# One decode layer: the end of the program moves from SyncE to TensorE

## The chip, the core and the metric

The kernel runs on one core of a Trainium2 chip. The core has five instruction streams: TensorE (PE for its matmuls, PEld for its weight loads), VectorE (DVE), ScalarE (ACT), GpSimd (POOL) and SyncE (SP). A letter q behind a name, as in SPq, means the engine's sequencer: DMA issues, waits and semaphore instructions, which are not counted as busy time. The metric is the device time of one execution in microseconds (us).

## What is computed

The reference adds three things: the input row x, a windowed attention over cached keys and values, and a gated feed-forward layer. Both of the latter read the same normalized row.

```
xn = _layernorm(x)                                  # x: 1 x 1 x 1024
return x + _A_ref(xn, k_cache, v_cache, wq, wo)     # 32 heads of 128, 4 key/value heads
         + _B_ref(xn, w_gate, w_up, w_down)         # 1024 -> 3584 -> 1024, gelu(g) * u

# _A_ref: q = x @ wq; the last 4096 rows of the caches; softmax(q k^T / sqrt(128)) v; then @ wo
# _B_ref: h = gelu(x @ w_gate) * (x @ w_up); then h @ w_down
```

There is one token, so nearly all of the work is to read the weights and the cache window, 94 MB in 32-bit floats, and to multiply each of them once.

## The kernel before

SP reads the weights and caches into one ring of 32768 columns in SBUF, in the order wq, keys, values, w_gate, w_up, wo, w_down (the table `PLAN`, which also says whose place in the ring each transfer takes). TensorE and VectorE share the multiplication: some rows of each weight go through matmuls, the others through a multiply and add on VectorE (`add_scaled`). The last weight, w_down, comes in ever smaller pieces, and `downs` finishes the output from them. It adds the last matmuls to the sum in two halves, tiles `y` and `y_last`, and each half is written by two DMAs of 2 x 128 elements, four stores in all. Two of the stores are issued by SP and two by ACT. The last one of all, of the lower part of `y_last`, is issued by SP.

No scheduler stands between the code and the program. `Flow` records every operation with the tiles that it reads and writes, works out which semaphores each must wait for, and issues the operations in the order in which the code calls them (line 97 is an added wait, line 237 is the operation itself: every operation of the program stands at these two lines, so the profile is read by tile names). The semaphores of DMAs are named flow_d_ and the operation's number, those of engines flow_e_ and the engine. In the built program the four stores have the semaphores flow_d_861 (number 138, SP), flow_d_862 (139, ACT), flow_d_866 (140, ACT) and flow_d_870 (145, SP, the last).

Behind the last store, `finish` leaves all semaphores at zero for the next execution. It does so in five steps on one engine, SP. It waits until `mark`, the first addition into `y`, is done (by then nobody waits for the loads' semaphores any more), and clears the first 36 semaphores with one range clear (line 210). It waits for the three earlier stores (line 212), and clears the next ten with a second range clear (line 213). Then it waits for the last store and takes that store's 16 back (line 214). The order in the numbers comes from the constructor: loads that nobody needs any longer stand first, the last store's semaphore stands last.

Behind `finish` the program ends on each engine. What the runtime then does is not among the program's instructions.

Of the kernel before, what the change touches and what calls it, by code (L numbers as in the profile page):

```python
# [36 lines left out]
SIZES = {"tp": NB, "acc": 2 * NB, "part": 8 * NB, "rows": 2 * NB}  # L37


def bits(dims):  # L40
    total = 1
    for step, count in dims:
        if step:
            grown = 0
            for i in range(count):
                grown |= total << (step * i)
            total = grown
    return total


class Flow:
# [4 lines left out]
    def __init__(self, nc, plan=None):  # L56
        self.nc = nc
        self.plan, self.idle = plan or (None, [])
        self.ops = []
        self.touched = {}  # L60
        self.sems = {}
        if self.plan:
            inc = self.plan[-1][1]
            self.last = inc
            used = {key for waits, _ in self.plan for key, _ in waits}
            used.update(inc for _, inc in self.plan if inc is not None)
            rest = sorted(used - {*self.idle, inc})
            for key in [*self.idle, *rest, inc]:
                self.sem(key)
        self.first = None  # L70
        for name in ("tensor", "vector", "scalar", "gpsimd", "sync"):
            setattr(self, name, Queue(self, getattr(nc, name)))
# [6 lines left out]
    @staticmethod  # L79
    def place(access):  # L80
        tensor = access.bass_ap.tensor
        if tensor.space == bass.MemoryType.DRAM:
            return None
        row = math.prod(list(tensor.shape)[1:])
        dims = [tuple(x) for x in access.ap]
        first, col = divmod(access.offset, row)
        parts = bits([(step // row, count) for step, count in dims if step >= row]) << first
        rest = [(step, count) for step, count in dims if step < row]
        if tensor.space == bass.MemoryType.PSUM:
            return tensor.name, (1 << 128) - 1, bits_of_banks(bits(rest) << col)  # L90
        return tensor.name, parts, bits(rest) << col
# [106 lines left out]
    def finish(self, mark, stores):  # L198

        end = self.nc.sync
        if not self.plan:
            return
        numbers = [s.num for s in self.sems.values()]
        first, cut, last = min(numbers), min(numbers) + len(self.idle), max(numbers)
        assert numbers == list(range(first, last + 1))
        assert stores[-1] == len(self.plan) - 1
        end.wait_ge(self.sem(self.plan[mark][1]), self.ticks(mark))
        end.sem_clear(range(first, cut))  # L210
        for k in stores[:-1]:
            end.wait_ge(self.sem(("d", k)), 16)
        end.sem_clear(range(cut, last))
        end.wait_ge(self.sem(self.last), 16).then_inc(self.sem(self.last), -16)

# [649 lines left out]
```

## Time and profile before

| what | value |
|---|---|
| time, median of 3 runs | 226.24 us (226.08 to 226.28) |
| time of the profiled execution | 226.24 us |
| its span, from the first to the last instruction of the program | 224.9 us |
| around the span (the difference) | 1.3 us |
| PE, PEld, DVE, ACT, POOL busy | 124.4, 65.4, 112.2, 28.0, 2.8 us |
| read from HBM | 94.38 MB, 420 GB/s over the span |

The span begins with the first and ends with the last instruction of the program on any engine; the 1.3 us are what the time of the execution has beyond it. Idle time stands in brackets behind a row, with the work that ended it. Times within the span are in us from its start.

### The profile page before, as it was taken

Reading aid. Unit: us, or ns where it says so; the run is one execution under the profiler, and the core shown is the slowest. Engines: PE = TensorE matmul, PEld = TensorE weight load, DVE = VectorE, ACT = ScalarE, POOL = GpSimd, SP = SyncE. Lnnn points to the kernel's source line nnn. Section 1 sums busy time; section 2 is a strip of 40 time slices with the busy share of each in tenths; the row PEclk is TensorE's granted clock in tenths of the full one; section 3 lists DMA queues with packets and bytes.
Section 4 is the critical chain, followed back from the end, with each engine's and each line's share of the span. In section 5 each row is a group of like instructions: output and inputs, shape, how many; then the busy total and the mean of one; then the engine's idle time right before and its main releaser. Section 6 shows DMA issues by size and latency. Waiting matters only on the chain.

```text
span 224.9 us, 2512 instructions
## 1 busy us (share of the span) xinstructions
PE 124.4 (55%) x1107; PEld 65.4 (29%) x1107; DVE 112.2 (50%) x142; ACT 28.0 (12%) x54; POOL 2.8 (1%) x9
## 2 busy tenths in 40 slices
PE   0120900557799860989848562235308988700986
PEld 0010200102654710754711110001004986300442
DVE  7030920592235082245049589239708933990942
ACT  2030000002435500445500310000000000000000
POOL 3000000000000000000000000000000000010000
PEclk9999995587999998599976958559955755755599
DMA  9889889799997999999989999989989989999994
GB/s 373 374 373 560 373 373 560 321 426 463 439 490 338 417 455 446 396 468 428 472 350 454 423 459 439 479 388 420 481 385 443 478 385 461 434 396 396 426 403 172
DMA packets 3193, 94.53 MB, mean 420 GB/s; under 512 B 446, under 2 KB 718, under 8 KB 1040
## 3 DMA queue, kind: packets, MB, share of 16 engines
q1 hardware_dynamic: 3160, 94.38, 97.8%
q8 instruction: 8, 0.13, 0.2%
q10 hardware_dynamic: 24, 0.01, 0.0%
q14 instruction: 1, 0.01, 0.0%
HBM read 94.38 MB, written 0.00 MB: 420 GB/s over the span
## 4 chain that ended last, share of the span: by engine, by line
DMA 67%; DVE 20%; PE 9%; SPq 1%; ACT 1%; issue 1%; POOL 0%; DVEq 0%
DMA ring<-in_B_w_gate 26%; DMA ring<-in_A_wq 18%; DMA ring<-in_A_wo 13%; DVE part L237 13%; DMA ring<-in_B_w_down 10%; PE tp L237 6%; DVE out_part L237 3%; PE out L237 3%; DVE rows L237 2%; SPq L237 1%; DVE g_sb L237 1%; ACT kT L237 1%; DVE hz L237 1%; PE acc L237 0%; DVE kT L237 0%
## 5 line engine op out<-in xcount | busy, mean ns | idle before, releaser
L237 PE MATMUL acc<-ring,xz 128*32 128x512 f32 x176 | 33.1, 850 | 39.3 <-DMA ring<-in_A_wq 23.0
L237 DVE SCALAR_TENSOR_TENSOR part<-ring,xz,part 128x3584 f32<-128x3584 f32 (+1 forms) x9 | 37.2, 4130 | 22.0 <-DMA ring<-in_A_wq 12.5
L237 PE MATMUL tp<-ident,ring 128*128 128x128 f32 x128 | 20.5, 310 | 8.9 <-DMA ring<-in_A_k_cache 6.1
L237 PEld LDWEIGHTS acc<-ring,xz 128*32 128x32 f32 x176 | 7.2, 145 | 60.3 <-issue 26.3
L237 DVE SCALAR_TENSOR_TENSOR out_part<-ring,oz,out_part 128x1024 f32<-128x1024 f32 x16 | 20.6, 1285 | 0.6
L237 PE MATMUL out<-ring,hz 128*32 128x256 f32 x168 | 12.8, 466 | 13.9 <-DMA ring<-in_B_w_down 13.9
L237 PEld LDWEIGHTS tp<-ident,ring 128*128 128x128 f32 x128 | 15.4, 155 | 16.9 <-DMA ring<-in_A_k_cache 7.0
L237 DVE COPY kT<-tp 128x512 f32<-128x512 f32 x12 | 8.1, 690 | 19.9 <-PE tp L237 19.9
L237 PE MATMUL out<-ring,oz 128*32 128x256 f32 x120 | 10.9, 541 | 9.6 <-DMA ring<-in_A_wo 9.6
L237 ACT ACTIVATE kT<-tp 128x512 f32<-128x512 f32 x20 | 11.4, 595 | 26.9 <-PE tp L237 26.9
L237 PE MATMUL tp<-ident,kT 128*128 128x4 f32 (+4 forms) x64 | 13.4, 343 | 1.6 <-DVE hz L237 1.6
L237 PEld LDWEIGHTS tp<-ident,kT 128*128 128x128 f32 (+2 forms) x64 | 13.1, 294 | 2.2 <-DVE hz L237 1.8
L237 DVE TENSOR_SCALAR part<-ring,xz 128x3584 f32<-128x3584 f32 (+1 forms) x3 | 6.5, 2172 | 13.7 <-DMA ring<-in_A_wq 7.6
L237 PEld LDWEIGHTS out<-ring,hz 128*32 128x32 f32 x168 | 5.8, 131 | 20.8 <-DMA ring<-in_B_w_down 16.1
L237 PE MATMUL acc<-part,units 128*32 128x512 f32 x44 | 7.1, 731 | 7.2 <-DVE part L237 7.2
L237 DVE SCALAR_TENSOR_TENSOR out_part<-ring,hz,out_part 128x1024 f32<-128x1024 f32 x6 | 7.7, 1284 | 5.6 <-DMA ring<-in_B_w_down 5.5
L237 PEld LDWEIGHTS out<-ring,oz 128*32 128x32 f32 x120 | 5.2, 154 | 15.3 <-DMA ring<-in_A_wo 10.5
L237 PE MATMUL o<-ring,pT 128*32 128x128 f32 x256 | 8.0, 274 | 1.1 <-ACT pT L237 1.0
L237 DVE TENSOR_REDUCE m<-s 128x2 f32<-128x1024 f32 x4 | 4.9, 1224 | 6.1 <-PE s L237 6.1
L237 PE MATMUL s<-kT,qz 128*32 128x512 f32 x64 | 7.7, 598 | 0.0
L237 PEld LDWEIGHTS o<-ring,pT 128*32 128x32 f32 x256 | 6.8, 110 | 2.2 <-ACT pT L237 1.9
L237 PE MATMUL tp<-ident,x_rows 2*128 2x2 f32 x4 | 0.6, 252 | 10.3 <-DMA x_rows<-in_A_x 10.3
(96 smaller groups left out, 73.5 us busy)
## 6 DMA issues: line engine op xcount, KB each, us to landing
ring<-in_B_w_gate SPq DMA_DIRECT2D x2, 7168.0 KB, 29.4
ring<-in_A_k_cache SPq DMA_DIRECT2D x4, 2048.0 KB, 19.7
ring<-in_A_v_cache SPq DMA_DIRECT2D x2, 4096.0 KB, 26.8
ring<-in_B_w_up SPq DMA_DIRECT2D x2, 3584.0 KB, 21.6
ring<-in_B_w_up SPq DMA_DIRECT2D x1, 7168.0 KB, 26.0
ring<-in_B_w_down SPq DMA_DIRECT2D x2, 2048.0 KB, 21.4
ring<-in_B_w_down SPq DMA_DIRECT2D x2, 512.0 KB, 21.9
ring<-in_B_w_down SPq DMA_DIRECT2D x2, 256.0 KB, 21.9
```

The lines of the kernel that those rows point to most:

```text
L237: return lambda *a, **k: self.flow.issue(self.engine, lambda: call(*a, **k))
```

## The change

One engine's stream gets the end of another's. The five steps of `finish` are issued on TensorE in place of SP. Since SP issues the last store and the second range clear must not come ahead of that, there is a new semaphore, `ISSUED` (flow_s_0, number 145 in the changed program, and the last store's becomes 146). SP adds one to it behind its last store, and TensorE waits for it ahead of its second range clear, which now covers 11 semaphores, 135 to 145, in place of 10.

```
+ISSUED = ("s", 0)
...
-            for key in [*self.idle, *rest, inc]:
+            for key in [*self.idle, *rest, ISSUED, inc]:
                 self.sem(key)
...
-        end = self.nc.sync
+        end = self.nc.tensor
...
+        self.nc.sync.sem_inc(self.sem(ISSUED), 1)
         end.wait_ge(self.sem(self.plan[mark][1]), self.ticks(mark))
         end.sem_clear(range(first, cut))
         for k in stores[:-1]:
             end.wait_ge(self.sem(("d", k)), 16)
+        end.wait_ge(self.sem(ISSUED), 1)
         end.sem_clear(range(cut, last))
         end.wait_ge(self.sem(self.last), 16).then_inc(self.sem(self.last), -16)
```

These are SP's last instructions before the change: the last pieces of w_down, SP's two stores, and the two range clears (ISA) with what they and the waits ahead of them wait for. Instructions that only wait or only count are not rows of this listing, so the last wait of line 214 is not seen.

```order
L237 DMA ring<-in_B_w_down 128x1024 [waits flow_e_PE]
L237 DMA ring<-in_B_w_down 128x512 [waits flow_e_DVE]
L237 DMA ring<-in_B_w_down 128x256 x2
L237 DMA out_y<-y 2x128 [waits flow_e_DVE]
L237 DMA out_y<-y_last 2x128 [waits flow_e_DVE]
L210 ISA [waits flow_e_DVE]
L213 ISA [waits flow_d_866,flow_d_862,flow_d_861]
```

The same place on SP after the change (all line numbers are five higher):

```order
L242 DMA ring<-in_B_w_down 128x1024 [waits flow_e_PE]
L242 DMA ring<-in_B_w_down 128x512 [waits flow_e_DVE]
L242 DMA ring<-in_B_w_down 128x256 x2
L242 DMA out_y<-y 2x128 [waits flow_e_DVE]
L242 DMA out_y<-y_last 2x128 [waits flow_e_DVE]
```

SP's stream ends with its store and the count on `ISSUED` behind it. On TensorE, the program ended with the last matmuls of w_down:

```order
L237 MATMUL tp<-ring,hz 32x128 [waits flow_d_756]
L237 MATMUL tp<-ring,hz 32x128 x3
L237 MATMUL acc<-ring,hz 32x128 [waits flow_d_757]
L237 MATMUL acc<-ring,hz 32x128
L237 MATMUL acc<-ring,hz 32x128 [waits flow_d_758]
L237 MATMUL acc<-ring,hz 32x128
```

After the change the two range clears stand behind them, and the second one has four waits in place of three:

```order
L242 MATMUL acc<-ring,hz 32x128 [waits flow_d_757]
L242 MATMUL acc<-ring,hz 32x128
L242 MATMUL acc<-ring,hz 32x128 [waits flow_d_758]
L242 MATMUL acc<-ring,hz 32x128
L214 ISA [waits flow_e_DVE]
L218 ISA [waits flow_d_866,flow_s_0,flow_d_862,flow_d_861]
```

The four waits are spread over three instructions: one that waits for flow_d_866 alone, one for flow_s_0 and flow_d_862, and the range clear itself, which waits for flow_d_861. Nothing else in the order of any engine differs.

More of the change, by code (lines that the diff above doesn't have):

```diff
@@ L37 @@
 SIZES = {"tp": NB, "acc": 2 * NB, "part": 8 * NB, "rows": 2 * NB}
+ISSUED = ("s", 0)
 def bits(dims):
@@ L67, in __init__ @@
             rest = sorted(used - {*self.idle, inc})
-            for key in [*self.idle, *rest, inc]:
+            for key in [*self.idle, *rest, ISSUED, inc]:
                 self.sem(key)
@@ L198, in finish @@
     def finish(self, mark, stores):
-        end = self.nc.sync
+        end = self.nc.tensor
         if not self.plan:
@@ L208, in finish @@
         assert stores[-1] == len(self.plan) - 1
+        self.nc.sync.sem_inc(self.sem(ISSUED), 1)
         end.wait_ge(self.sem(self.plan[mark][1]), self.ticks(mark))
@@ L212, in finish @@
             end.wait_ge(self.sem(("d", k)), 16)
+        end.wait_ge(self.sem(ISSUED), 1)
         end.sem_clear(range(cut, last))
```

## The prediction

> **What bounds the kernel now.** I read the page's chain first, then the stretches, then the last three microseconds instruction by instruction. The chain, by engine and by line, and the busiest DMA queue say what the time goes to:
>
> ```profile
> DMA 67%; DVE 20%; PE 9%; SPq 1%; ACT 1%; issue 1%; POOL 0%; DVEq 0%
> q1 hardware_dynamic: 3160, 94.38, 97.8%
> ```
>
> The 16 DMA engines are busy for 97.8% of the span with SP's loads. The change touches none of these; it works behind the last store. So the second view is a table of three stretches (PE, PEld, DVE, ACT and POOL busy time with instruction counts, granted clock, DMA share, GB/s):
>
> ```profile
> 0.00:221.60 221.60, 122.67 (x1083) 64.84 (x1084) 110.91 (x138) 27.98 (x54) 2.79 (x9) 0.78 0.99 426
> 221.60:224.00 2.40, 1.70 (x24) 0.60 (x24) 1.24 (x4) 0.00 (x0) 0.00 (x0) 1.00 0.16 55
> 224.00:224.90 0.90, 0.00 (x0) 0.00 (x0) 0.00 (x0) 0.00 (x0) 0.00 (x0) 1.00 0.01 2
> ```
>
> Until 221.60 the kernel is bound by DMA (share 0.99). From 224.00 no engine computes and hardly a byte moves: 0.90 us of pure latency. There the change is at work, and in the 226.24 - 224.9 = 1.3 us that the time has beyond the span. The timeline shows what comes just before:
>
> ```profile
> 222.62 0.68 PE L237 MATMUL acc<-ring,hz 128*32 128x128 f32 x8
> ...
> 223.08 0.60 DVE L237 TENSOR_TENSOR y_last<-y,acc 64x128 f32<-64x128 f32 x2
> ...
> 223.46 0.28 ACTq L237 DMA_DIRECT2D out_y<-y_last  x1
> 223.71 0.26 SPq L237 DMA_DIRECT2D out_y<-y_last  x1
> ```
>
> TensorE is done at 222.62 + 0.68 = 223.30, VectorE at 223.68; SP has issued the last store at 223.97. What SP does then stands in its lines one by one (duration in ns, then the start in us), and the third row is its only wait there:
>
> ```profile
> L210 SPq EVENT_SEMAPHORE_RANGE_CLEAR  x1: 92/92/92, 224.0 to 224.0; - x1
> L212 SPq EVENT_SEMAPHORE  x1: 28/28/28, 224.7 to 224.7; - x1
> SPq L212 <- DMA out_y<-y_last: 0.5, 1, 0.5
> L213 SPq EVENT_SEMAPHORE_RANGE_CLEAR  x1: 42/42/42, 224.7 to 224.7; - x1
> L214 SPq EVENT_SEMAPHORE  x1: 17/17/17, 224.8 to 224.8; - x1
> ```
>
> So the first clear lies under the flight of the stores. SP waits 0.5 us for ACT's second store, clears ten semaphores, and the last store's landing ends the program. These rows are rounded to 0.1 us. The trace also keeps when each semaphore was written; its records, in ns from the start of the span, are these (2 is a semaphore that the program does not use, 3 to 53, 54 to 104, 105 to 155, 156 to 206 and 207 to 255 are zeroed in five blocks behind the program's end):
>
> ```
> 140 (ACT's second store, landed)      224636
> 145 (the last store, landed)          224821     taken back by SP  224855
> 135 to 144 (SP's second clear)        224732 ... 224746
> 2   before the first instruction      -371 -337 -299 -255 -231 -119 -80 -46 0
> 2   at the end                        223490 224403 224441 224485 225004 | 225048 225087 225121 225168
> 207 to 255 zeroed                     225127 ... 225214
> 7 to 53 zeroed                        225419 ... 225764
> 2   once more                         225988 226023 226061 226104 226128 | 226227 226265 226299 226346
> ```
>
> Semaphore 2 counts a meeting of the five engines, up and back down: nine updates each time. Who stands where is read from the program's first instructions, which follow the first meeting:
>
> ```profile
> L853 SPq DRAIN  x1: 7/7/7, 0.0 to 0.0; - x1
> L853 DVEq DRAIN  x1: 10/10/10, 0.1 to 0.1; - x1
> L853 POOLq INC_SWDGE_SEM  x1: 27/27/27, 0.1 to 0.1; - x1
> L853 ACTq DRAIN  x1: 8/8/8, 0.1 to 0.1; - x1
> L853 PEldq DRAIN  x1: 8/8/8, 0.3 to 0.3; - x1
> ```
>
> SP starts first and PE last. So I read the order as PE, ACT, POOL, DVE, SP going up, and DVE, POOL, ACT, PE coming back. At the end PE came to it at 223490, 0.19 us behind its last matmul; ACT, POOL and DVE follow at 224403 to 224485; SP, at the turn, comes at 225004, 0.15 us behind its last instruction. Only the way back, 164 ns to PE at 225168, is left then.
>
> **The change, step by step.** The sum is made against the profiled execution, 226.24 us, which is also the median shown.
>
> First clear, 36 semaphores. It leaves SP (92 ns) and goes to PE, which has been idle since 223.30. Its wait, for the first addition into `y`, was met at 222.74. Even at the slowest pace that the records show, (225764 - 225419) / 46 = 7.5 ns a semaphore, it takes 0.3 us and ends by 223.7, under the wait for ACT's store to 224.64. Cost: nothing; the cover is the 0.9 us of flight.
>
> `ISSUED`. SP adds one behind its store at 223.97: one instruction of 17 ns, seen by about 224.07. If SP had to wait for its store as ACT does on its way to the meeting (0.66 us from 223.74 to 224403), it would come at 224.63, still no later than ACT's landing. Cost: nothing, but the cover is then used up.
>
> PE's waits. How PE executes a wait is shown by the added waits in the program:
>
> ```profile
> L97 SPq EVENT_SEMAPHORE  x11: 17/17/17, 26.4 to 195.9; - x11
> L97 PEldq EVENT_SEMAPHORE  x8: 51/51/51, 10.2 to 219.9; - x8
> L853 SPq EVENT_SEMAPHORE  x1: 17/17/17, 0.7 to 0.7; - x1
> L853 PEldq EVENT_SEMAPHORE  x1: 51/51/51, 0.7 to 0.7; - x1
> ```
>
> 51 ns on PE against 17 on SP. The records give 29 ns from the write of a semaphore to PE's start (SP 17), and 76 ns from one wait's start to that of the next instruction. ACT's store lands at 224.636, so PE's first wait starts at 224.665, the second at 224.741, the clear at 224.817. On SP the clear started at 224.72, with one wait less ahead of it.
>
> The second clear. No row shows a range clear on PE. By SP's row it is 42 ns and costs nothing more; by the pace of 7.5 ns for 11 semaphores, plus SP's fixed 28 ns (42 less the 14 in which its ten are written) taken up to three times, 110 to 165 ns. I take 130, since 3 to 53 are the block that PE, the last one released, would zero. The last wait then starts at 224.98 with a short step between, and ends at 225.03. The last store has landed at 224.82, so it is no longer the last thing waited for. The span becomes 225.03 in place of 224.86: +0.17 (bounds +0.08 with SP's clear, +0.21 with the slow one).
>
> The meeting. PE now comes last, and it stands at the start of the way up. Its step from its last instruction to its arrival I take as 0.16 us, like SP's 0.15 and PE's own 0.19 behind its last matmul (bounds 0.15 and 0.22; the latter is 225764 to 225988). Then follows the whole way up and back: 0 - (-371) = 371 ns in the first meeting, 226346 - 225988 = 358 in the last; before, it was 164 of it. That is +0.19 to +0.21 us more. I take +0.20.
>
> Sum: 0.17 + 0.01 + 0.20 = +0.38 us, 226.24 + 0.38 = 226.62. The bounds add up to 0.08 + 0.00 + 0.19 = 0.27 and 0.21 + 0.07 + 0.21 = 0.49, thus 226.51 to 226.73. All of it is late next at PE's release, which already zeroed its block last, from 225419 to 225764.
>
> [...]
>
> **The rivals.** 0.2% of 226.24 us is 0.45 us, about what a measurement of this kernel can tell from no change; the forecast lies just under that.
>
> The end of the time does not hang on PE's release. If the time ends with something that only needs the last engine's arrival, the +0.20 is not paid, and the store's landing may even cover the clear: 226.24 + 0.08 to 0.17, about 226.3 to 226.4. Against it: the time ends 1.3 us behind the span, at a point past the zeroing that waits for the release.
>
> PE's end is dearer than SP's by more than the rows show: each of the five instructions at a price between its measured 51 ns and a slow clear, a longer step to the meeting, and the first steps of PE behind its release (251 ns from 225168 to 225419, SP's 123) paid again. One more such step of 0.1 to 0.25 us gives 226.7 to 226.9, over the bound. For it: PE has the slowest of every step in the records. It decides from 0.07 us beyond the forecast.
>
> The other side: SP is set free early. A fetch of instructions starts as SP comes to the meeting; the row has the queue's packets, MB and share, and the record of this one is a start at 225034 and a duration of 493 ns:
>
> ```profile
> q14 instruction: 1, 0.01, 0.0%
> ```
>
> If the fetch, done at 225.53, is what holds the last meeting, then SP, arriving at about 224.64, has it done 0.37 us earlier, and the time falls to 226.24 - 0.37 + 0.08 = 225.95. It decides only if something waits for the fetch beyond 225.53. Against it: PE's zeroing lasts until 225.76, after the fetch, and would be later.
>
> **How the numbers follow.** The forecast, up to the bound of 226.69: 0.48. The end that does not hang on the release, 226.25 to 226.45: 0.12. PE dearer, above 226.69: 0.34, a third of it beyond 226.9, since one unshown instruction form on the path may cost what no row bounds. SP set free: 0.06. The predicted time is the forecast's, 226.62. The range goes from 226.25 to 226.95; it leaves out the 0.06 below and about 0.10 above. Faster by over 0.2% is 0.06; within 0.2% is 0.48 + 0.12 = 0.60; slower is 0.34.
>
> **What would show it.** In the changed profile the second clear stands on PE at about 224.8, 0.1 us later than on SP, and takes over 100 ns. The last wait starts later than the last store's landing, and the span is about 225.0. PE's first clear ends before 224. SP's last row is its count at about 224.0. Semaphore 2 has no early update any more: PE writes the first of the nine, behind the end of the span, and 0.36 us pass from it to the last. The zeroing of 7 to 53 starts about 0.4 us later. The prediction is wrong if the clear on PE is as quick as on SP and the way up costs nothing (226.3), if PE takes much longer than 0.16 us to the meeting, or if anything ahead of 221.6 differs, since the change issues nothing there.

## The result, and the profile after

The change made the kernel slightly slower: 226.74 us at the median against 226.24 us before, a ratio of 1.0022 (95% interval 1.0014 to 1.0030). One execution of twelve took 348 us and is left out of the ratio; without it the median is 226.72. The profiled execution took 226.70 us, with a span of 225.1 us.

The table of stretches, now to 225.10 (columns as before), shows where the time did not come from. The 221.60 us under the loads are as they were, with a DMA share of 0.99. The stretch in which nothing computes grew from 0.90 to 1.10 us:

```profile
0.00:221.60 221.60, 121.75 (x1087) 64.22 (x1091) 110.91 (x138) 27.97 (x54) 2.80 (x9) 0.79 0.99 426
221.60:224.00 2.40, 1.62 (x24) 0.54 (x24) 1.22 (x4) 0.00 (x0) 0.00 (x0) 1.00 0.14 48
224.00:225.10 1.10, 0.00 (x0) 0.00 (x0) 0.00 (x0) 0.00 (x0) 0.00 (x0) 1.00 0.03 9
```

The timeline shows the same matmuls and stores, 0.06 to 0.08 us earlier in this execution:

```profile
222.54 0.68 PE L242 MATMUL acc<-ring,hz 128*32 128x128 f32 x8
...
223.40 0.28 ACTq L242 DMA_DIRECT2D out_y<-y_last  x1
223.63 0.26 SPq L242 DMA_DIRECT2D out_y<-y_last  x1
```

Line by line, the end of the program now stands on PE (duration in ns, then the start in us). SP's only instruction behind its store is the first row:

```profile
L212 SPq EVENT_SEMAPHORE  x1: 17/17/17, 223.9 to 223.9; - x1
L214 PEldq EVENT_SEMAPHORE_RANGE_CLEAR  x1: 305/305/305, 222.8 to 222.8; - x1
L216 PEldq EVENT_SEMAPHORE  x1: 51/51/51, 224.6 to 224.6; - x1
L217 PEldq EVENT_SEMAPHORE  x1: 51/51/51, 224.7 to 224.7; - x1
L218 PEldq EVENT_SEMAPHORE_RANGE_CLEAR  x1: 121/121/121, 224.8 to 224.8; - x1
L219 PEldq EVENT_SEMAPHORE  x1: 51/51/51, 225.0 to 225.0; - x1
```

The second range clear takes 121 ns on PE for 11 semaphores, where SP took 42 for ten, and the last wait starts at 225.0. The trace's records of semaphore writes and instruction starts give this to the nanosecond:

```
140 (ACT's second store, landed)    224582
PE: first wait, second wait, clear  224610, 224716, 224822 (ends 224943)
146 (the last store, landed)        224760
PE: last wait                       225034 (ends 225085)
2   at the end                      225314 225349 225387 225430 225454 | 225551 225589 225625 225672
7 to 53 zeroed                      225886 ... 226234
2   once more                       226458 226492 226530 226574 226598 | 226696 226734 226769 226815
```

The last store had landed 274 ns before PE turned to it. From there on all is late: PE comes to the meeting first of nine updates, and all of the way up and back follows.

Counted from the last store's landing, so that an earlier or later landing drops out, the time divides into five stages (ns). "End" is the end of the program's last instruction; "step" is from there to that engine's update of semaphore 2; "way" is from there to the last of the nine updates; "zeroing" is from there to the first of PE's zeroed semaphores; "rest" runs to the last of all updates. Which engine an update or a zeroed block belongs to is inferred. Five of the nine updates lie behind the program's last instruction where that is SP's, all nine where it is PE's. The block 7 to 53 (3 to 6 have no record) is taken as PE's: it starts last, and its 7.5 ns a semaphore are near the pace at which PE's own first range clear wrote its 36, (223090 - 222846) / 35 = 7.0, where SP's took (224098 - 224040) / 35 = 1.7.

| kernel | end | step | way | zeroing | rest | sum |
|---|---|---|---|---|---|---|
| before | 34 | 149 | 164 | 251 | 927 | 1525 |
| after | 325 | 229 | 358 | 214 | 929 | 2055 |

The difference is 530 ns, and the profiled landing was 61 ns earlier than before, which leaves 469. The times of these two executions differ by 0.46 us. In every profiled execution of this study the time is the last update of semaphore 2 less 0.10 to 0.12 us (before 226.24 against 226.346, after 226.70 against 226.815). So the time ends with the last meeting, and these stages account for what the change did between these two executions.

### The profile page after: what moved, and what is told of

Its sections match the earlier page's. It is cut to its first block, busy times and chain, and to the rows that moved or that the text cites. A ratio compares the mean times of both kernels' runs of the same rounds, so it can differ in the third digit from the quotient of the medians.

```text
span 225.1 us, 2514 instructions
## 1 busy us (share of the span) xinstructions
PE 123.4 (55%) x1107; PEld 64.8 (29%) x1107; DVE 112.1 (50%) x142; ACT 28.0 (12%) x54; POOL 2.8 (1%) x9
## 4 chain that ended last, share of the span: by engine, by line
DMA 67%; DVE 20%; PE 9%; SPq 1%; ACT 1%; issue 1%; POOL 0%; DVEq 0%
DMA ring<-in_B_w_gate 26%; DMA ring<-in_A_wq 18%; DMA ring<-in_A_wo 13%; DVE part L242 13%; DMA ring<-in_B_w_down 10%; PE tp L242 6%; DVE out_part L242 3%; PE out L242 2%; DVE rows L242 2%; SPq L242 1%; DVE g_sb L242 1%; ACT kT L242 1%; DVE hz L242 1%; PE acc L242 0%; DVE kT L242 0%
## 5 line engine op out<-in xcount | busy, mean ns | idle before, releaser
L242 PE MATMUL acc<-ring,xz 128*32 128x512 f32 x176 | 34.7, 883 | 42.7 <-DMA ring<-in_A_wq 23.6
L242 PE MATMUL acc<-part,units 128*32 128x512 f32 x44 | 5.8, 599 | 6.4 <-DVE part L242 6.4
```

Source lines behind the costliest of these rows:

```text
L242: return lambda *a, **k: self.flow.issue(self.engine, lambda: call(*a, **k))
```

## The experiments

Two theories were set against each other. By the first, the place of the last engine in the meeting costs, beside the speed of its instructions. By the second, PE's slow instructions are all. The table of stages for all kernels stands at the end of this section. The stages are read from one profiled execution of each kernel; the times are medians of all, each beside the kernel before on the same chip.

### Only the last wait on TensorE

SP keeps its waits and both range clears:

```
-        end.wait_ge(self.sem(self.last), 16).then_inc(self.sem(self.last), -16)
+        self.nc.tensor.wait_ge(self.sem(self.last), 16).then_inc(self.sem(self.last), -16)
```

> SP keeps both range clears and the three earlier waits; TensorE only waits for the last store and takes its 16 back. Theory 1 (the place in the meeting costs, whatever PE does before): the end of the span is 0.05 us later against the last store's landing than before (29 + 51 ns on PE in place of 17 + 17 on SP), PE's step to the meeting is 229 ns in place of 149, the way up and back 358 in place of 164, PE's release to its zeroing 214 in place of 251: +0.05 + 0.08 + 0.19 - 0.04 = +0.28 us, 226.52. Theory 2 (PE's slow waits and clears behind ACT's store are all of it): only the 0.05 remains, 226.3.

Measured: 226.52 against 226.24 us, ratio 1.0013 (1.0004 to 1.0022). PE has one instruction behind its matmuls:

```profile
L213 SPq EVENT_SEMAPHORE_RANGE_CLEAR  x1: 42/42/42, 224.6 to 224.6; - x1
L214 PEldq EVENT_SEMAPHORE  x1: 51/51/51, 224.7 to 224.7; - x1
```

The stages sum to 1811 ns, 286 more than before, where 0.28 us was expected. The span ends only 45 ns later against the landing. What is paid lies outside the span, where the page shows nothing: 86 ns in the step and 192 in the way. The theory that PE's slow chain is all of it falls.

### The late store waited for last

In the changed kernel the waits were put in another order. The wait that the code names first ends up in the range clear itself (flow_d_861 in the changed kernel), and the others in two instructions ahead of it. So ACT's second store, which lands last of the three, is now named first, and the two instructions ahead no longer wait for it:

```
-        for k in stores[:-1]:
-            end.wait_ge(self.sem(("d", k)), 16)
+        end.wait_ge(self.sem(("d", stores[2])), 16)
         end.wait_ge(self.sem(ISSUED), 1)
+        for k in stores[:2]:
+            end.wait_ge(self.sem(("d", k)), 16)
```

> The changed kernel with its waits in another order: the store that lands last of the three (ACT's second) is waited for by the range clear itself, the two others and ISSUED by the two waits ahead. Theory 1: the clear starts 29 ns behind that landing in place of 240, so that the chain is 0.21 us shorter and still just longer than the last store's flight: 226.74 - 0.21 = 226.53. If only the place in the meeting counts, and the chain does not: 226.74, no change to the changed kernel.

Measured: 226.52 against 226.24 us, ratio 1.0016 (1.0007 to 1.0025). The two waits start at 224.4 and 224.5, the clear at 224.6:

```profile
L218 PEldq EVENT_SEMAPHORE  x2: 51/51/51, 224.4 to 224.5; - x2
L219 PEldq EVENT_SEMAPHORE_RANGE_CLEAR  x1: 121/121/121, 224.6 to 224.6; - x1
L220 PEldq EVENT_SEMAPHORE  x1: 51/51/51, 224.8 to 224.8; - x1
```

The clear starts at 224.644, 59 ns behind the landing of ACT's second store in place of 240; 29 were expected, but the second wait starts at 224.538 and the clear follows it by 106. The program ends 115 ns behind the landing of the last store in place of 325. These 210 ns come from the order of the waits alone, and they come back in the time (226.74 to 226.52). Both shares of the loss are real: the chain of waits and the place in the meeting.

### The clears on TensorE, the last wait on SP

```
-        end.wait_ge(self.sem(self.last), 16).then_inc(self.sem(self.last), -16)
+        self.nc.sync.wait_ge(self.sem(self.last), 16).then_inc(self.sem(self.last), -16)
```

> TensorE has both range clears and the waits ahead of them, SP waits for its own last store and takes the 16 back. Theory 1: SP comes to the meeting as before, but PE, first on the way up, comes behind its clear: clear's end 183 ns behind the last store's landing, a step of 229, and 358 for the whole way, against 183 and 164 before: +0.42 - 0.04 = +0.38 us, 226.62. A theory by which the last wait on PE is what costs says no change, 226.24; one by which the end of the span decides says +0.15, 226.4.

Measured: 226.57 against 226.24 us, ratio 1.0016 (1.0007 to 1.0025). SP is done with the last store as early as before (end 34 ns behind the landing), yet the time is 0.33 us longer, because PE, at the foot of the way up, is still clearing:

```profile
L218 PEldq EVENT_SEMAPHORE_RANGE_CLEAR  x1: 121/121/121, 224.9 to 224.9; - x1
L219 SPq EVENT_SEMAPHORE  x1: 17/17/17, 224.8 to 224.8; - x1
```

The stages sum to 346 ns more than before, against 380 expected; PE's step behind a range clear was 193 ns, not 229. So the loss does not need the last wait on PE: it is enough that PE comes late to the meeting.

### The end on the three other engines

The changed kernel with `end` on ScalarE, GpSimd or VectorE:

```
-        end = self.nc.tensor
+        end = self.nc.scalar    # or gpsimd, or vector
```

> The changed kernel with ScalarE in place of TensorE. Theory 1 (place): ACT is second on the way up, 323 ns from the end of the meeting in place of SP's 164, thus +0.16 us, and its waits take 17 ns as SP's do, so that its chain ends with the last store's landing or up to 0.1 behind it: 226.40 to 226.50. Theory 2 (PE is slow, the place is free): 226.24 to 226.34.

> The changed kernel with GpSimd in place of TensorE. By the place in the meeting (third on the way up, 285 ns from there to the end in place of 164): +0.12 us and whatever its chain of waits ends behind the last store's landing, 0.0 to 0.15: 226.36 to 226.51. If only PE's slowness counts: 226.24 to 226.39.

> The changed kernel with VectorE in place of TensorE. By the place in the meeting (fourth on the way up, 241 ns from there to the end in place of 164): +0.08 us; its waits for two semaphores take 50 ns at a distance of 98, so its chain ends 0.1 to 0.25 us behind the last store's landing: 226.40 to 226.57. If the place is free: 226.34 to 226.49. The profile decides: the second half of the nine updates of semaphore 2, counted from VectorE's arrival, takes 241 ns or 164.

Measured: ScalarE 226.34 against 226.24 (ratio 1.0009, 1.0000 to 1.0018), GpSimd 226.81 against 226.17 (1.0026, 1.0015 to 1.0038), VectorE 226.48 against 226.17 (1.0013, 1.0004 to 1.0022).

The way from the last engine's arrival to the end of the meeting was 323 ns from ACT, 282 from POOL, 242 from DVE, 358 from PE and 164 from SP. It falls with the place on the way up, as the order PE, ACT, POOL, DVE, SP demands, and this order had been read from the program's start alone. The expected values were 323, 285 and 241. By the stages ACT costs 225 ns and DVE 235, within what was expected. By its median ACT was a miss: 226.34 lies below the expected 226.40 to 226.50, at the upper end of what the second theory gave (226.24 to 226.34), and only the interval (0 to 0.41 us) allows the 225 ns. What speaks for the place is the way of 323 ns, and the time beyond the span, 1.52 us on average against 1.36 (last column of the table). POOL was a miss: 652 ns in place of 120 to 270. Its instructions are quick,

```profile
L218 POOLq EVENT_SEMAPHORE_RANGE_CLEAR  x1: 89/89/89, 224.7 to 224.7; - x1
L219 POOLq EVENT_SEMAPHORE  x1: 17/17/17, 224.9 to 224.9; - x1
```

but its step from the last of them to the meeting was 567 ns.

### Only the last wait on GpSimd, or on ScalarE

This is the first experiment's edit with `self.nc.gpsimd` or `self.nc.scalar`.

> SP keeps both range clears, GpSimd alone waits for the last store and takes its 16 back. With the whole end on GpSimd its step from its last instruction to the meeting was 567 ns, four times SP's 149. If that step is GpSimd's own whatever stands ahead of it: the end of the span 0.04 us behind the last landing, 0.57 us to the meeting, 282 ns from third place, release to zeroing about 220: 0.04 + 0.57 + 0.28 + 0.22 = 1.11 against 0.03 + 0.15 + 0.16 + 0.25 = 0.60 before, +0.51 us, 226.70. If the step came from the range clears on GpSimd shortly before: 0.15 in place of 0.57, +0.09 us, 226.3.

> SP keeps both range clears, ScalarE alone waits for the last store and takes its 16 back. ScalarE had a step of 134 ns to the meeting and 323 from second place on. The sum of stages: 0.04 + 0.13 + 0.32 + 0.22 = 0.71 against 0.60 before, +0.12 us, 226.33. If the place in the meeting were free, the span alone would count: no change, 226.24 to 226.25. The profile decides, since the difference is close to what the times can tell: the stretch from the last store's landing to the last update of semaphore 2 is 1.53 us before, 1.65 by the sum of stages.

Measured: GpSimd 226.73 against 226.25 us (1.0023, 1.0013 to 1.0033), ScalarE 226.83 against 226.25 (1.0026, 1.0015 to 1.0036). GpSimd's step is 572 ns with one instruction behind the stores and 567 with five, so neither the range clears nor the number of its instructions makes it; why GpSimd needs it stays open. ScalarE was a miss. The way is 322 ns as expected, but the step is 587 ns, where it had been 134 with the whole end on ScalarE. The row of its last instruction is as short as ever:

```profile
L214 ACTq EVENT_SEMAPHORE  x1: 17/17/17, 224.6 to 224.6; - x1
```

### Where ScalarE loses its time

First, four needless waits for the same store ahead of ScalarE's last one. The trace shows up to two waits in one instruction, so these are three instructions in place of one:

```
+        for _ in range(4):
+            self.nc.scalar.wait_ge(self.sem(self.last), 16)
         self.nc.scalar.wait_ge(self.sem(self.last), 16).then_inc(self.sem(self.last), -16)
```

> As with ScalarE's single wait for the last store, with two needless waits for the same store ahead of it on ScalarE, three instructions in place of one. ScalarE's step from its last instruction to the meeting was 587 ns with one instruction behind its stores and 134 with five, two of them range clears. If the step falls with the number of instructions (where the program's end lies in the instruction stream): somewhere from 134 to 587, a step down of at least 0.1 us between one, three and five. If it takes a range clear or an early instruction on ScalarE to have a short step: 587 still.

Measured, in one execution: 226.91 against 226.04 us. The step falls to 147 ns. The loss had moved: the first of the three starts at 224.886, the next one 370 ns later, and the third 76 ns behind that.

```profile
L215 ACTq EVENT_SEMAPHORE  x2: 17/28/38, 224.9 to 225.3; - x2
L216 ACTq EVENT_SEMAPHORE  x1: 38/38/38, 225.3 to 225.3; - x1
```

So the loss does not belong to the end of the program. It comes once, behind the first instruction after ScalarE's stores. (The same with five instructions in place of three was planned and has no result.) To tell whether it belongs to that instruction or to a place in ScalarE's stream, four needless instructions (eight waits) were put far ahead, before the stores, with one last wait as in the run that lost 587 ns:

```
+        for _ in range(8 if nc.plan else 0):
+            nc.nc.scalar.wait_ge(nc.sem(("e", "Activation")), 1)
         tiles = [loaded["d", i][:, n * D:(n + 1) * D] for i in range(3) for n in range(DOWN[i])]
```

> As with ScalarE's single wait for the last store, with four needless instructions more on ScalarE some 20 us earlier, ahead of its stores, where it has nothing to do (each waits for a count of its own that was reached long ago). In the run with needless waits behind the stores ScalarE lost 0.37 us after the first instruction behind its stores, and only 147 ns from the last to the meeting. If that loss has its place in ScalarE's instruction stream, a certain number of instructions from its start, it now falls ahead of the stores, into a wait: 0.13 to 0.15 us from the last instruction to the meeting, and the time 226.33 to 226.45. If it belongs to the first instruction behind the stores wherever that stands: 0.59 us still, 226.83.

Measured: 226.50 against 226.20 us, ratio 1.0015 (1.0005 to 1.0024); the median is 0.05 us above what was expected. The step is 137 ns, and the stages sum to 115 ns more than before, as first expected of ScalarE (0.12 us). The median's 0.30 us is more than that: the span was 0.16 us longer too, on average over the executions (225.01 against 224.85). The program ends 37 ns behind the last landing (34 before), so this part came ahead of the landing. Why is open.

The needless instructions ran at 131.4 to 132.0 us, 91 us ahead of the stores and not some 20 as expected:

```profile
L750 ACTq EVENT_SEMAPHORE  x4: 38/38/38, 131.4 to 132.0; - x4
```

A loss of the same size shows among them. They start at 131.439, 131.520, 131.597 and 131.988 us: steps of 81 and 77 ns, then one of 391. In the trace's records of ScalarE this gap stands behind its 63rd instruction. So it does in the two earlier runs: there the 63rd instruction is the first of the three waits, with 370 ns behind it where 60 follow a single wait elsewhere (all on ACT), and the one last wait, with 587 ns behind it. With the whole end on ScalarE the 63rd is the first range clear, over at 224.05, and the next instruction waits until 224.74 anyway, which hides the loss. So the loss has a place in the instruction stream, counted in instructions. With it a fetch of 8 KB of instructions moved: it starts at 225.67 us in the run with the loss, and at 135.28 us with four instructions more. Whether ScalarE waits for a fetch there, or for something else at that place, stays open, since the fetch that the trace records comes after the loss, not during it.

### All stages

| kernel | end | step | way | zeroing | rest | sum | against before | beyond the span, us (executions) |
|---|---|---|---|---|---|---|---|---|
| before (SP) | 34 | 149 | 164 | 251 | 927 | 1525 | | 1.36 (33) |
| after (PE) | 325 | 229 | 358 | 214 | 929 | 2055 | +530 | 1.62 (11) |
| only the last wait on PE | 79 | 235 | 356 | 211 | 930 | 1811 | +286 | 1.65 (11) |
| PE, the late store last | 115 | 230 | 358 | 216 | 928 | 1847 | +322 | 1.64 (11) |
| clears on PE, last wait on SP | 182 | 193 | 358 | 209 | 929 | 1871 | +346 | 1.59 (11) |
| all on ACT | 115 | 134 | 323 | 219 | 959 | 1750 | +225 | 1.52 (11) |
| all on DVE | 191 | 182 | 242 | 216 | 929 | 1760 | +235 | 1.47 (11) |
| all on POOL | 149 | 567 | 282 | 221 | 958 | 2177 | +652 | 1.90 (7) |
| only the last wait on POOL | 41 | 572 | 285 | 219 | 956 | 2073 | +548 | 1.91 (10) |
| only the last wait on ACT | 38 | 587 | 322 | 218 | 927 | 2092 | +567 | 1.97 (8) |
| the same, two waits ahead | 504 | 147 | 322 | 247 | 928 | 2148 | +623 | 1.51 (1) |
| the same, four early instructions | 37 | 137 | 322 | 215 | 929 | 1640 | +115 | 1.52 (10) |

The last column checks the stages of one execution against all executions of a kernel: it is the mean of the time less the span. Beside the kernel before it grows by what step, way, zeroing and rest together grow, to within 0.05 us. Two small differences in the table have no explanation here: the zeroing (251 and 247 ns in two kernels, 209 to 221 in the others) and the rest (956 to 959 in three kernels, 927 to 930 in the others).

No kernel of the study does better than the one before. With the whole end on one engine SP has the shortest chain, 34 ns behind the last landing against 115 to 325, and it stands at the turn of the meeting, with a way of 164 ns against 242 to 358.

## Why the prediction was right, and where its sizes were off

The time came out slower, within the range, 0.12 us beyond the predicted 226.62. The forecast's case ended at 226.69; with 226.74 and a ratio of 1.0022 the result lies a hair on the other side, in the rival "PE's end is dearer", which had a chance of 0.34 against the forecast's 0.48. The interval reaches to both sides of 1.002. The sum's own upper bound, 226.73, is passed by a hair too; the wider range is that of the rivals.

- **The first clear costs nothing**: right. It took 305 ns on PE, as the slowest pace had it (0.3 us), and was over at 223.12. It came earlier than forecast: it started at 222.82, ahead of the end of PE's last matmul at 223.22 and not behind it.
- **`ISSUED` costs nothing**: right. SP counted at 223.93, and PE came to that wait at 224.72.
- **PE's waits**: the mechanism was right, the price low. The first wait started 28 ns behind ACT's landing (29 taken), but wait follows wait at 106 ns, not 76. The 76 stood for a wait followed by a weight load. This term is 60 ns short over two waits.
- **The second clear**: 121 ns, where 130 was taken between bounds of 42 and 165. But the next instruction starts 91 ns behind its end (61 where the late store is waited for last), and a short step of some 30 was assumed. Together, the program's end is 0.29 us later against the landing, where the sum had 0.17 and its upper bound 0.21.
- **The step to the meeting**: 229 ns, where 160 was taken and 220 was the upper bound. PE's own 0.19 us behind its last matmul was a poor stand-in: the first clear started on PE at 222.82, 0.4 us before the end that the trace gives that matmul, 223.22.
- **The meeting**: right. 358 ns of way in place of 164, 0.19 us, 0.20 taken. The runs on the other engines bear out the order of the five.
- **Not foreseen**: PE starts zeroing 214 ns behind its release, 251 before. That gives 0.04 us back. It is not because PE came last: with the end on ACT, DVE or POOL it came first and waited, and took 216 to 221. This was luck for the forecast, as it hides a part of what the other terms lack.

In sum +0.29 + 0.08 + 0.19 - 0.04 = +0.53 us at an equal landing, where the forecast was 0.17 + 0.01 + 0.20 = +0.38. The terms that were mis-sized are the two that rest on PE's own sequencer. These are two of the three prices of the rival "PE's end is dearer"; the third, PE's first steps behind its release, went the other way. The rival by which the end does not hang on PE's release falls, since the time is the last update of semaphore 2 less 0.10 to 0.12 us in every profiled execution. The rival by which SP is set free early had the fetch on the wrong engine: with SP done at 223.95 the fetch still started at 225.08, and it moved when ScalarE had four instructions more and SP the same.

## What to carry to other kernels

In these runs it mattered beyond its last instruction which engine finishes the program last: the rest of the way through the closing meeting was 164 ns for SP and 358 for PE. So here the last wait and the clean-up belong on SP, which stands at the turn and has the shortest instructions (42 ns for the second range clear, of ten semaphores, where the others took 81 to 121 for eleven), and no other engine should be late there either: with the clears alone on PE the time was 0.33 us longer. On PE, where one wait followed the other at 106 ns, the event that comes last should be waited for by the last of them: that alone was 0.21 us.

## What was not expected of the hardware

A range clear took very different times on the engines: for the 36 semaphores 92 ns on SP and 305 to 308 on PE. With the whole end on each, ScalarE took 185, GpSimd 226 and VectorE 251.

GpSimd took 567 and 572 ns from its last instruction to the meeting, the others 134 to 235 (ScalarE without its loss). And ScalarE lost 0.31 to 0.45 us at one place of its instruction stream, behind its 63rd recorded instruction (370 and 391 ns where the usual steps are 60 and 77, and 587 in place of 137). With a single wait on ScalarE this place was on the path that sets the end; four instructions more ahead of it moved the place to where ScalarE had time to spare.
